# First FFN products on half tiles over four column blocks, and attention of batch 1 behind the w3@w_out blocks

## The chip, the cores and the metric

The kernel runs on one core of a Trainium2 chip. The metric is the time of one execution on the device in microseconds; the medians are over the runs given with them. A profiled execution also has a *span*, from its first to its last instruction, which is about 2 us shorter than its time. The kernel before takes 260.06 us; the execution whose profile is read here took 259.7 us (span 257.9).

Engine names in the profile: PE is TensorE (matmuls and transposes), PEld its weight loads, DVE is VectorE, ACT is ScalarE, POOL is GpSimd, SP is SyncE. L344 is line 344 of that kernel's own file, so one line of code has different numbers in different kernels.

## The reference

```python
# attention, for each of 8 batches and 8 heads; S = 576, D = 64
phi(x) = concat(relu(x) * cos(theta), relu(x) * sin(theta))     # 128 features
kv  = phi(k)^T @ v            # 128 x 64
z   = sum_s phi(k)            # 128
x   = (phi(q) @ kv) / (phi(q) @ z + 1e-6)
# FFN on 4608 tokens: model width 512, inner width 1024
out = ((x @ w1) * (x @ w2) @ w3) @ w_out
```

Inputs and outputs are float32; the kernel computes in bf16 and folds `w3 @ w_out` into one 1024 x 512 matrix, w34, while it runs. The FFN works on tiles of 512 tokens, nine in all: tile 0 needs four of the five chunks of queries of batch 0, and tile 1 needs the fifth and chunks of batch 1.

## The kernel before

Each chunk of 128 queries goes through a chain of three engines: q transpose (PE), copy, numerator (PE), normalisation (DVE), x transpose (PE), copy to xT (ACT). Ahead of it, DVE makes the cosine half and ACT the sine half of phi (`qp` in the profile). The sums `kv` and `z` of a batch are copied out of PSUM into `kvs`, half by ACT and half by DVE, before its first numerator.

```python
def num(b, c):                       # numerator and normalisation of one chunk
    ...
    for h in range(H):
        nc.tensor.matmul(nt[:, h // 4, ds((h % 4) * 65, 65)], lhsT=qpT[:, h, ds(at, 128)],
                         rhs=kvs[:, h, :], start=True, stop=True)
    nc.vector.tensor_scalar_add(out=den[rows], in0=n4[:, :, :, 64], scalar1=1e-6)
    nc.vector.reciprocal(out=den[rows], in_=den[rows])
    nc.vector.tensor_tensor(out=xblk[rows], in0=n4[:, :, :, 0:D], in1=den..., op=ALU.mult)

def x_tr(b, c):                      # for batches 0 and 1
    for kc in range(4):
        nc.tensor.transpose(pst[:, kc, 0:R], xf[:, ts(kc, 128)], identb[rows, rows])
    nc.scalar.copy(out=xT[t][:, :, ds(o, R)], in_=pst[:, 0:4, 0:R])
```

The FFN is a generator that stops after each group of four 512-column matmuls (0.865 us of PE). Whatever lies in the slot of that number is emitted there, so a slot number is a place in PE's instruction order. Tile 0 has 24 slots; the eight w3@w_out blocks, two halves each, lie in slot 15 and have places 0 to 15 of their own, after which places 16 to 23 are the output groups of tile 0. The parts that the change touches:

```python
if t == 0:                           # first products: two column blocks, token quarters
    for group in (((0, 0),), ((0, 1), (1, 0)), ((1, 1), (0, 2), (1, 2)), ((0, 3), (1, 3))):
        ...
for jp in range(4): load_w3(jp)      # loads: batch 1 lies between the blocks of w3
load(1, "k"); load_w3(4); load(1, "v"); load_w3(5); load(1, "q"); load_w3(6); load_w3(7)
...
attention_at(1, between, kv=(7, 8, 8, 9, 9), tr=(10, 11, 13, 15, 17),
             nu=(12, 14, 16, 18, 20), xt=(14, 16, 18, 20, 22))
```

In the last line, `nu` are the places of the five numerators and `xt` those of the five x transposes: each transpose is two places behind its numerator.

## Time and profile before

| stage of the kernel before | from | to | what happens in it |
|---|---|---|---|
| start | 0 | 9.78 us | loads, idle matmuls (the first 7 start 0.43 us apart, the later ones 0.216) |
| opening | 9.78 | 21.15 us | attention of batch 0; PE waits for other engines |
| rest of tile 0 | 21.15 | 65.62 us | FFN, w3@w_out, attention of batch 1; PE without gaps |
| tile 1 | 65.62 | 84.05 us (products) | FFN, attention of batch 2; PE without gaps |
| tiles 1 to 8 | 84.05 | 257.9 us | the same, in steady state |

PE sets the time: 96% busy, and 91% of the chain that ended last. The prediction below shows these lines and the chain of the opening. Two more lines of the timeline of the kernel before are needed as marks. Columns are start, length, engine, line, operation, output and inputs, shapes, and a bracket with idle time and its releaser if PE was idle before it.

```profile
35.77 0.61 PE L199 MATMUL pst<-identb,w3b 128*128 128x128 bf16 x8
...
65.62 1.03 PE L391 MATMUL ffnps<-xT,w1b 128*128 128x512 bf16 x4
```

The first is the transpose of the second w3 block (call it the **w3 mark**: all first FFN products lie ahead of it), the second the first product of tile 1 (the **tile 1 mark**). Comparing these two marks between kernels tells in which stage time was won or lost. One caution: a kernel that leaves some of this work for behind a mark reaches the mark earlier by as much. The changed kernel leaves the numerator and the x transpose of chunk 3 of batch 1 (0.26 + 0.22 us of PE) to tile 1.

### The profile page before, as it was taken

The numbers are of one execution on the slowest core, as the hardware profiler recorded it, in microseconds if no ns is written. First come the engines' busy times: TensorE is split into PE (matmuls) and PEld (weight loads), VectorE is DVE, ScalarE is ACT, GpSimd is POOL, SyncE is SP. The second block draws the span as 40 slices with busy tenths as digits, with TensorE's granted clock in tenths as the row PEclk, the third lists the DMA queues.
The fourth block names the chain that finished last, engine by engine and source line by source line (L and its number), as shares of the span: only waits on it lengthen the run. The fifth ranks groups of instructions, "written<-read, shape, count | busy, mean of one in ns | idle before, by whom it ended". The sixth has DMA issues, their size and how long they took to land.

```text
span 257.9 us, 5056 instructions
## 1 busy us (share of the span) xinstructions
PE 248.3 (96%) x1954; PEld 134.0 (52%) x1954; DVE 147.0 (57%) x344; ACT 128.3 (50%) x219; POOL 84.3 (33%) x144
## 2 busy tenths in 40 slices
PE   8778999999999999999999999999999999999992
PEld 3467455665555455546554654555455544444442
DVE  6785557569699538834972687178516613313320
ACT  2765327639955546545655465646533233323322
POOL 7752244440690374048205900610140031022000
PEclk9999999999999999999999999999999999999999
DMA  7999999999599999988998999826490252014015
GB/s 194 184 196 206 210 201 203 201 198 199 165 153 178 152 170 190 165 164 147 195 160 173 173 198 124 185 62 122 93 205 11 46 123 78 0 37 128 0 43 122
DMA packets 66968, 37.10 MB, mean 144 GB/s; under 512 B 35584, under 2 KB 63488, under 8 KB 66944
## 3 DMA queue, kind: packets, MB, share of 16 engines
q0 software_dynamic: 34432, 27.20, 64.5%
q1 hardware_dynamic: 32352, 9.44, 20.7%
q8 instruction: 15, 0.25, 0.4%
q10 hardware_dynamic: 160, 0.13, 0.2%
q14 instruction: 9, 0.07, 0.1%
HBM read 38.80 MB, written 9.44 MB: 187 GB/s over the span
## 4 chain that ended last, share of the span: by engine, by line
PE 91%; DMA 3%; DVE 2%; ACT 1%; issue 1%; ACTq 0%; POOLq 0%
PE ffnps L391 47%; PE ffnps L421 23%; PE ffnps L211 5%; PE pst L297 4%; PE pnum L315 4%; PE pnum L268 3%; DMA vs<-in_v_dram 3%; PE pst L199 1%; DVE xblk L322 1%; PE pst L344 1%; DVE qpT L299 1%; PE ffnps L438 0%; PE kva L285 0%; ACT osb L440 0%; DVE den L320 0%
## 5 line engine op out<-in xcount | busy, mean ns | idle before, releaser
L416 DVE TENSOR_TENSOR abT<-asb,ffnps 128x512 bf16<-128x512 bf16 x70 | 47.8, 683 | 69.7 <-PE ffnps L391 66.4
L391 PE MATMUL ffnps<-xT,w1b 128*128 128x512 bf16 (+1 forms) x312 | 74.9, 362 | 0.7 <-DVE xblk L322 0.6
L391 PE MATMUL ffnps<-xT,w2b 128*128 128x512 bf16 (+1 forms) x312 | 74.9, 362 | 0.0
L412 ACT CAST asb<-ffnps 128x512 bf16<-128x512 f32 x70 | 41.0, 586 | 64.8 <-PE ffnps L391 57.9
L421 PE MATMUL ffnps<-w34b,abT 128*128 128x512 bf16 x280 | 63.7, 379 | 0.0
L383 POOL DMA_DIRECT2D out_dram<-osb x42 | 22.3, 536 | 122.5 <-ACT osb L427 122.5
L391 PEld LDWEIGHTS <-w1b 128*128 128x128 bf16 x312 | 28.0, 98 | 28.4 <-issue 1.0
L421 PEld LDWEIGHTS <-abT 128*128 128x128 bf16 x280 | 26.7, 98 | 30.2
L391 PEld LDWEIGHTS <-w2b 128*128 128x128 bf16 x312 | 26.9, 97 | 23.9
L427 ACT COPY osb<-ffnps 128x512 f32<-128x512 f32 x35 | 20.5, 585 | 36.6 <-PE ffnps L421 36.6
L244 ACT ACTIVATE qp<-qs,sinv 128x512 bf16<-128x512 bf16 (+1 forms) x40 | 28.4, 721 | 0.8 <-DMA qs<-in_q_dram 0.8
L322 DVE TENSOR_TENSOR xblk<-pnum,den 128x512 bf16<-128x512 f32 (+1 forms) x38 | 26.2, 691 | 1.3
L244 ACT ACTIVATE kp<-ks,sinv 128x512 bf16<-128x512 bf16 (+1 forms) x35 | 24.7, 721 | 0.0
L315 PEld LDWEIGHTS <-qpT 128*128 128x128 bf16 x320 | 15.1, 98 | 8.0 <-DVE qpT L299 0.3
L242 DVE TENSOR_SCALAR qp<-qs,cosv 128x512 bf16<-128x512 bf16 (+1 forms) x40 | 18.5, 474 | 0.3 <-DMA qs<-in_q_dram 0.3
L260 POOL COPY va<-vs 128x512 bf16<-128x512 bf16 (+1 forms) x30 | 18.6, 645 | 0.0
L299 DVE COPY qpT<-pst 128x1024 bf16<-128x1024 bf16 (+1 forms) x22 | 13.7, 626 | 5.0 <-PE pst L297 4.7
L315 PE MATMUL pnum<-kvs,qpT 128*128 128x65 bf16 x304 | 16.0, 194 | 0.0
L297 PEld LDWEIGHTS <-qp 128*128 128x128 bf16 x192 | 12.5, 98 | 6.6 <-ACT qp L244 1.8
L211 PE MATMUL ffnps<-woutb,w3T 128*128 128x512 bf16 x64 | 15.8, 379 | 0.0
L268 PEld LDWEIGHTS <-kp 128*128 128x128 bf16 x280 | 12.9, 98 | 5.4
L297 PE MATMUL pst<-identb,qp 128*128 128x128 bf16 x192 | 14.6, 219 | 1.1 <-ACT qp L244 0.5
(73 smaller groups left out, 174.0 us busy)
## 6 DMA issues: line engine op xcount, KB each, us to landing
out_dram<-osb POOLq DMA_DIRECT2D x16, 256.0 KB, 3.4
out_dram<-osb POOLq DMA_DIRECT2D x24, 128.0 KB, 3.1
qs<-in_q_dram POOLq DMA_DIRECT2D x9, 256.0 KB, 7.7
ks<-in_k_dram POOLq DMA_DIRECT2D x7, 320.0 KB, 6.3
vs<-in_v_dram POOLq DMA_DIRECT2D x7, 320.0 KB, 8.3
qs<-in_q_dram POOLq DMA_DIRECT2D x7, 320.0 KB, 6.8
w3b<-in_moe_w_dram POOLq DMA_DIRECT2D x8, 256.0 KB, 15.3
ks<-in_k_dram POOLq DMA_DIRECT2D x7, 256.0 KB, 7.0
```

What stands on the lines that cost most here:

```text
L211: nc.tensor.matmul(acc[:, :], lhsT=w3T[:, lc, :], rhs=woutb[:, lc, :], start=(lc == 0), stop=(lc == 7))
L244: nc.scalar.activation(out=dst[:R, c, :, D:F], in_=src[:R, :, c, :], func=ACTF.Relu, scale=sinv[:R, at:at + 1], bias=0.0)
L268: nc.tensor.matmul(kvt[:, h // 4, ds((h % 4) * 65, 65)], lhsT=kp[:, c, h, :], rhs=va[:, c, h, 0:D + 1], start=(i == 0 and h % 4 == 0), sto ...
L297: nc.tensor.transpose(pst[:, h, :], qp[:, c, h, :], identb[:])
L315: nc.tensor.matmul(nt[:, h // 4, ds((h % 4) * 65, 65)], lhsT=qpT[:, h, ds(at, 128)], rhs=kvs[:, h, :], start=True, stop=True)
L322: nc.vector.tensor_tensor(out=xblk[rows], in0=n4[:, :, :, 0:D], in1=den[rows].unsqueeze(3).to_broadcast([R, 2, 4, D]), op=ALU.mult)
L383: on.dma_start(out=rows[:, :, cols], in_=osb[64 * i:64 * i + rows.shape[0], :, cols])
L391: nc.tensor.matmul(out_ps[:, tok], lhsT=w[:, kc, ts(jc, 128)], rhs=x[:, kc, tok], start=(kc == 0), stop=(kc == 3))
L412: nc.scalar.copy(out=asb[:], in_=aT[:, :])
L416: nc.vector.tensor_mul(out=abT[:, jc, :], in0=asb[:], in1=bT[:, :])
L421: nc.tensor.matmul(ops[:, :], lhsT=abT[:, jc, ts(ms, 128)], rhs=w34b[:, jc, :], start=(jc == 0), stop=(jc == 7))
L427: nc.scalar.copy(out=osb[:, ms % 2, :], in_=ops[:, :])
```

## The change

The intent: let the first FFN product start as soon as one chunk of tokens is normalised, cover the waits for later chunks with more products (four column blocks instead of two, on half tiles of 256 tokens), and get attention of batch 1 out of the way of the w3@w_out blocks, so that those need only w3 itself. Its core, with cuts (the comments are the document's):

```diff
-    idle_mms(28)
+    idle_mms(31)
 ...
-    for jp in range(4):
+    for jp in range(8):
         load_w3(jp)
-    load(1, "k")
-    load_w3(4)
-    load(1, "v")
-    load_w3(5)
-    load(1, "q")
-    load_w3(6)
-    load_w3(7)
+        if jp == 4:
+            load(1, "k")
+    load(1, "qv")
 ...
         if t == 0:
-            acc = [ps_ffn.tile([P, 512], FP32, name="ffnps") for _ in range(4)]
-            for group in (((0, 0),), ((0, 1), (1, 0)), ((1, 1), (0, 2), (1, 2)), ((0, 3), (1, 3))):
-                ...
-        for jc in range(2 if t == 0 else 0, 8):
+            yield from on_half(0)       # per half: column blocks 0, 1 in quarters of 128 tokens,
+            yield from on_half(1)       # then blocks 2, 3 on 256 tokens
+        for jc in range(4 if t == 0 else 0, 8):
 ...
-            spread(prep_units(1, (prep_k,)), 2, 4, between)
-            spread(prep_units(1, (prep_v,)), 5, 7, between)
-            spread(prep_units(1, (prep_q,)), 8, 11, between)
-            attention_at(1, between, kv=(7, 8, 8, 9, 9), tr=(10, 11, 13, 15, 17),
-                         nu=(12, 14, 16, 18, 20), xt=(14, 16, 18, 20, 22))
+            spread(prep_units(1, (prep_k,)), 8, 10, between)
+            spread(prep_units(1, (prep_q,)), 13, 15, between)
+            spread(prep_units(1, (prep_v,)), 15, 16, between)
+            attention_at(1, between, kv=(16, 16, 17, 17, 18), tr=(14, 15, 15, 16, 17),
+                         nu=(19, 20, 21, 22, 24), xt=(20, 21, 22, 23, 25))
 ...
-            spread(prep_units(2), 17, 23, slots)
+            spread(prep_units(2, (prep_k,)), 20, 23, slots)
+        elif t == 1:
+            # the rest of batch 1's attention, batch 2's q and v preparation in slots 0 to 4,
+            # batch 2's attention and batch 3's preparation a little later than before
```

Not shown: the order of the chunks' instructions ahead of the FFN (the sine half of chunk 0 goes before the kvs copy, idle matmuls stand elsewhere, the numerators use other PSUM pools), and the products' output banks.

More of the change, by code (lines that the diff above doesn't have):

```diff
@@ L96 @@
     ps_tr = ctx.enter_context(tc.tile_pool(name="ps_tr", bufs=2, space=bass.MemoryType.PSUM))
-    first = ctx.enter_context(ExitStack())
-    ps_first = first.enter_context(tc.tile_pool(name="ps_first", bufs=1, space=bass.MemoryType.PSUM))
+    first = [ctx.enter_context(ExitStack()) for _ in range(2)]
+    ps_idle = first[1].enter_context(tc.tile_pool(name="ps_idle", bufs=1, space=bass.MemoryType.PSUM))
+    ps_first = first[0].enter_context(tc.tile_pool(name="ps_first", bufs=1, space=bass.MemoryType.PSUM))
     ctx.enter_context(tc.manual_schedule())
@@ L159 @@
     nc.scalar.activation(out=tiny[:], in_=zeros[:, 0:1], func=ACTF.Relu, scale=1.0, bias=0.0)
-    unread = ps_first.tile([P, 512], FP32, name="unread")
-    kva = ps_first.tile([P, 512], FP32, name="kva")
+    unread = ps_idle.tile([P, 512], FP32, name="unread")
+    kva = ps_idle.tile([P, 512], FP32, name="kva")
     def idle_mms(n):
@@ L175 @@
     load_first(nc.gpsimd, q0, q, 2, 2)
-    for c0, n in ((0, 256), (256, 256), (512, 512)):
+    for c0, n in ((0, 256), (256, 256), (512, 256), (768, 256)):
         nc.gpsimd.dma_start(out=w1b[:, :, ds(c0, n)], in_=w1v[:, :, ds(c0, n)])
         nc.gpsimd.dma_start(out=w2b[:, :, ds(c0, n)], in_=w2v[:, :, ds(c0, n)])
-        if c0 == 0:
+        if c0 == 256:
             load_first4(nc.gpsimd, q0, q)
     nc.gpsimd.dma_start(out=woutb[:], in_=moe_w_out.rearrange("(c p) m -> p c m", p=P))
-    for jp in range(4):
+    for jp in range(8):
         load_w3(jp)
-    load(1, "k")
-    load_w3(4)
-    load(1, "v")
-    load_w3(5)
-    load(1, "q")
-    load_w3(6)
-    load_w3(7)
+        if jp == 4:
+            load(1, "k")
+    load(1, "qv")
     load(2, "kqv")
@@ L207, in w34_mm @@
         if part == 0:
-            w34_acc[jp] = ps_ffn.tile([P, 512], FP32, name="ffnps")
+            w34_acc[jp] = ffn_tile()
         acc, w3T = w34_acc[jp], w3Ts[jp]
@@ L237, in att_of, with features @@
         return att[b]
-    def features(b, dst, src, c):
+    def features(b, dst, src, c, cos=True, sin=True):
         R = ROWS[c]
         at = c if b == 0 else NCH + c
-        nc.vector.tensor_scalar(out=dst[:R, c, :, 0:D], in0=src[:R, :, c, :], scalar1=0.0,
-                                scalar2=cosv[:R, at:at + 1], op0=ALU.max, op1=ALU.mult)
-        nc.scalar.activation(out=dst[:R, c, :, D:F], in_=src[:R, :, c, :], func=ACTF.Relu,
-                             scale=sinv[:R, at:at + 1], bias=0.0)
+        if cos:
+            nc.vector.tensor_scalar(out=dst[:R, c, :, 0:D], in0=src[:R, :, c, :], scalar1=0.0,
+                                    scalar2=cosv[:R, at:at + 1], op0=ALU.max, op1=ALU.mult)
+        if sin:
+            nc.scalar.activation(out=dst[:R, c, :, D:F], in_=src[:R, :, c, :], func=ACTF.Relu,
+                                 scale=sinv[:R, at:at + 1], bias=0.0)
     def prep_k(b, c):
@@ L287, in kv_first @@
                                  stop=(c == NCH - 1 and h % 4 == 3))
+        att_of(0)["kvs"] = kvs
+        yield
         nc.scalar.copy(out=kvs[:, 0:4, :], in_=halves[0][:, 0:260])
         nc.vector.tensor_copy(out=kvs[:, 4:8, :], in_=halves[1][:, 0:260])
-        att_of(0)["kvs"] = kvs
+        yield
     def q_tr(b, c, evac=True):
@@ L309, in num @@
         qpT, kvs = att[b]["qpT"], att[b]["kvs"]
-        if b == 0 and c in (0, 2):
+        if b == 0 and c == 0:
             nt = ps_first.tile([P, 2, 512], FP32, name="pfirst")
@@ L383, in store, with ffn_tile @@
             on.dma_start(out=rows[:, :, cols], in_=osb[64 * i:64 * i + rows.shape[0], :, cols])
+    ffn_tiles = [0]
+    def ffn_tile():
+        pool = ps_ffn[ffn_tiles[0] // 2 % 2]
+        ffn_tiles[0] += 1
+        return pool.tile([P, 512], FP32, name="ffnps")
     def ffn_groups(t):
@@ L387, in ffn_groups, with products @@
         abT = fsb.tile([P, 8, 512], BF16, name="abT", bufs=2)
-        def products(out_ps, w, jc, tok):
+        def products(out, w, jc, tok):
             for kc in range(4):
-                nc.tensor.matmul(out_ps[:, tok], lhsT=w[:, kc, ts(jc, 128)], rhs=x[:, kc, tok],
+                nc.tensor.matmul(out, lhsT=w[:, kc, ts(jc, 128)], rhs=x[:, kc, tok],
                                  start=(kc == 0), stop=(kc == 3))
-        def to_abT(jc, aT, bT):
-            asb = fsb.tile([P, 512], BF16, name="asb")
-            nc.scalar.copy(out=asb[:], in_=aT[:, :])
-            nc.vector.tensor_mul(out=abT[:, jc, :], in0=asb[:], in1=bT[:, :])
@@ L399, in ffn_groups @@
-        if t == 0:
-            acc = [ps_ffn.tile([P, 512], FP32, name="ffnps") for _ in range(4)]
-            for group in (((0, 0),), ((0, 1), (1, 0)), ((1, 1), (0, 2), (1, 2)), ((0, 3), (1, 3))):
-                for jc, quarter in group:
-                    products(acc[2 * jc], w1b, jc, ts(quarter, 128))
-                    products(acc[2 * jc + 1], w2b, jc, ts(quarter, 128))
-                    if quarter == 3:
-                        to_abT(jc, acc[2 * jc], acc[2 * jc + 1])
-                yield
@@ L408, in ffn_groups, with on_half @@
-        for jc in range(2 if t == 0 else 0, 8):
-            aT = ps_ffn.tile([P, 512], FP32, name="ffnps")
-            products(aT, w1b, jc, slice(0, 512))
+        def on_half(half):
+            for pair in range(2):
+                a, b = ffn_tile(), ffn_tile()
+                if pair == 0:
+                    for quarter in range(2):
+                        for i in range(2):
+                            for ps, w in ((a, w1b), (b, w2b)):
+                                products(ps[:, ds(256 * i + 128 * quarter, 128)], w, i,
+                                         ds(256 * half + 128 * quarter, 128))
+                            if half == 0 and quarter == 0 and i == 0:
+                                yield
+                        if quarter == 0:
+                            yield
+                else:
+                    for ps, w in ((a, w1b), (b, w2b)):
+                        for i in range(2):
+                            products(ps[:, ts(i, 256)], w, 2 + i, ts(half, 256))
+                asb = fsb.tile([P, 512], BF16, name="asb")
+                nc.scalar.copy(out=asb[:], in_=a[:, :])
+                nc.vector.tensor_mul(out=abT[:, ts(pair, 2), ts(half, 256)],
+                                     in0=asb[:].rearrange("p (i n) -> p i n", i=2),
+                                     in1=b[:, :].rearrange("p (i n) -> p i n", i=2))
+                yield
@@ L411, in ffn_groups @@
+        if t == 0:
+            yield from on_half(0)
+            yield from on_half(1)
+        for jc in range(4 if t == 0 else 0, 8):
+            aT = ffn_tile()
+            products(aT[:, :], w1b, jc, slice(0, 512))
             asb = fsb.tile([P, 512], BF16, name="asb")
@@ L413, in ffn_groups @@
             yield
-            bT = ps_ffn.tile([P, 512], FP32, name="ffnps")
-            products(bT, w2b, jc, slice(0, 512))
+            bT = ffn_tile()
+            products(bT[:, :], w2b, jc, slice(0, 512))
             nc.vector.tensor_mul(out=abT[:, jc, :], in0=asb[:], in1=bT[:, :])
             yield
+        if t == 0:
+            yield
         for ms in range(3 if t == NT - 1 else 4):
-            ops = ps_ffn.tile([P, 512], FP32, name="ffnps")
+            ops = ffn_tile()
             for jc in range(8):
@@ L435, in ffn_groups @@
                 cols = ts(half, 256)
-                ops = ps_ffn.tile([P, 512], FP32, name="ffnps")
+                ops = ffn_tile()
                 for jc in range(8):
@@ L456 @@
         prep_v(0, c)
-    kv_first()
-    for c in range(2):
-        prep_q(0, c)
+    kv_steps = kv_first()
+    next(kv_steps)
+    prep_q(0, 0)
+    next(kv_steps)
+    prep_q(0, 1)
     idle_mms(2)
     q_tr(0, 0)
-    q_tr(0, 1)
-    for c in range(2, 4):
-        prep_q(0, c)
-    idle_mms(1)
+    prep_q(0, 2)
+    q_tr(0, 1, evac=False)[1]()
     num(0, 0)
-    q_tr(0, 2, evac=False)[1]()
-    idle_mms(1)
-    q_tr3 = q_tr(0, 3, evac=False)[1]
+    features(0, feat[0][1], raw[0, "q"], 3, sin=False)
+    idle_mms(3)
+    x_tr(0, 0)
     num(0, 1)
-    idle_mms(2)
-    x_tr(0, 0)
-    q_tr3()
-    num(0, 2)
-    x_tr(0, 1)
-    feature_buffers(1)
-    first.close()
-    ps_ffn = ctx.enter_context(tc.tile_pool(name="ps_ffn", bufs=4, space=bass.MemoryType.PSUM))
+    features(0, feat[0][1], raw[0, "q"], 3, cos=False)
+    q_tr(0, 2)
+    ps_ffn = []
+    for stack in first:
+        stack.close()
+    for i in range(2):
+        ps_ffn.append(ctx.enter_context(tc.tile_pool(name=f"ps_ffn{len(ps_ffn)}", bufs=2,
+                                                     space=bass.MemoryType.PSUM)))
     for t in range(NT):
@@ L482 @@
         if t == 0:
-            slots[0].append(lambda: num(0, 3))
-            slots[0].append(lambda: x_tr(0, 2))
-            slots[1].append(lambda: x_tr(0, 3))
-            slots[1].append(lambda: prep_q(0, 4))
-            slots[4].append(lambda: q_tr(0, 4))
-            slots[7].append(lambda: num(0, 4))
-            slots[9].append(lambda: x_tr(0, 4))
-            slots[14].append(lambda: w3_tr(0))
-            between = [[] for _ in range(32)]
-            spread(prep_units(1, (prep_k,)), 2, 4, between)
-            spread(prep_units(1, (prep_v,)), 5, 7, between)
-            spread(prep_units(1, (prep_q,)), 8, 11, between)
-            attention_at(1, between, kv=(7, 8, 8, 9, 9), tr=(10, 11, 13, 15, 17),
-                         nu=(12, 14, 16, 18, 20), xt=(14, 16, 18, 20, 22))
+            slots[0].append(lambda: x_tr(0, 1))
+            slots[1].append(lambda: num(0, 2))
+            slots[1].append(lambda: q_tr(0, 3, evac=False)[1]())
+            slots[2].append(lambda: x_tr(0, 2))
+            slots[2].append(lambda: num(0, 3))
+            slots[3].append(lambda: x_tr(0, 3))
+            slots[4].append(lambda: feature_buffers(1))
+            slots[5].append(lambda: prep_q(0, 4))
+            slots[7].append(lambda: q_tr(0, 4))
+            slots[9].append(lambda: num(0, 4))
+            slots[11].append(lambda: x_tr(0, 4))
+            slots[13].append(lambda: w3_tr(0))
+            between = [[] for _ in range(32)]
+            later = [[] for _ in range(24)]
+            spread(prep_units(1, (prep_k,)), 8, 10, between)
[3 more added lines that the diff above has]
+                         nu=(19, 20, 21, 22, 24), xt=(20, 21, 22, 23, 25))
+            later[:8] = between[24:32]
             for jp in range(8):
@@ L505 @@
             slots[16].append(lambda: load(3, "kqv"))
-            spread(prep_units(2), 17, 23, slots)
+            spread(prep_units(2, (prep_k,)), 20, 23, slots)
+        elif t == 1:
+            for g in range(24):
+                slots[g] += later[g]
+            spread(prep_units(2, (prep_q,)), 0, 4, slots)
+            spread(prep_units(2, (prep_v,)), 0, 4, slots)
+            attention_at(2, slots, kv=(2, 3, 4, 5, 6), tr=(3, 5, 7, 9, 11),
+                         nu=(8, 10, 12, 14, 17), xt=(8, 10, 12, 14, 17))
+            for g, name in ((1, "k"), (8, "q"), (15, "v")):
+                slots[g].append(lambda name=name: load(4, name))
+            each = [u for c in zip(*(prep_units(3)[i:i + NCH] for i in (0, 5, 10))) for u in c]
+            spread(each, 6, 23, slots)
         else:
```

## The prediction

> **What bounds the kernel now.** I read the page first (engine shares, the slices, the chain that ended last), then busy time in stretches I chose, then the timeline of the first 28 us and of the passage from token tile 0 to token tile 1. The two ends of the page say that TensorE (PE) is the bound:
>
> ```profile
> span 257.9 us, 5056 instructions
> PE 248.3 (96%) x1954; PEld 134.0 (52%) x1954; DVE 147.0 (57%) x344; ACT 128.3 (50%) x219; POOL 84.3 (33%) x144
> ...
> PE 91%; DMA 3%; DVE 2%; ACT 1%; issue 1%; ACTq 0%; POOLq 0%
> ```
>
> Busy PE is not yet full PE, so I cut the span at the last visible gap of the opening (21.15 us) and at the starts of tiles 1 and 2. Columns: stretch, its length, then busy time of PE, weight loads, DVE, ACT, POOL, clock, DMA.
>
> ```profile
> 9.78:21.15 11.37, 8.54 (x147) 6.80 (x146) 9.32 (x28) 6.70 (x11) 5.85 (x9) 1.00 1.51 195
> 21.15:65.62 44.47, 44.38 (x412) 26.73 (x413) 28.43 (x67) 24.85 (x44) 15.62 (x24) 1.00 1.31 204
> 65.62:84.05 18.43, 18.43 (x178) 10.77 (x177) 15.51 (x33) 12.49 (x23) 8.92 (x15) 1.00 1.02 158
> ```
>
> After 21.15 PE has almost no gap, and the work there is issued at full rate: eight 512-column matmuls of w3@w_out start at 36.21 and the next group at 37.94, so 1.73/8 = 216 ns each. In 9.78 to 21.15 PE idles 2.8 us and another 2 us of its busy time is idle matmuls on zeros or overlap of modelled ends. So this change has two questions: how many of these early microseconds it recovers, and whether it opens gaps in a stretch that has none. The waits of the opening are a latency chain per chunk of queries, seen in the timeline (start, length, engine, line, instruction):
>
> ```profile
> 15.68 0.42 PE L315 MATMUL pnum<-kvs,qpT 128*128 128x65 bf16 x8
> ...
> 16.13 0.17 DVE L319 TENSOR_SCALAR den<-pnum 128x8 f32<-128x8 f32 x1 [0.41 <-PE pnum L315]
> ...
> 16.34 0.20 DVE L320 RECIPROCAL den<-den 128x8 f32<-128x8 f32 x1
> ...
> 16.57 0.69 DVE L322 TENSOR_TENSOR xblk<-pnum,den 128x512 bf16<-128x512 f32 x1
> ...
> 18.45 0.38 PE L391 MATMUL ffnps<-xT,w1b 128*128 128x128 bf16 x4 [0.64 <-DVE xblk L322]
> ...
> 21.15 0.40 PE L344 MATMUL pst<-identb,xblk 128*128 128x128 bf16 x4 [0.72 <-DVE xblk L322]
> ```
>
> The reader should see that the numerator (L315) starts at 15.68 and its normalised block is complete at 16.57+0.69 = 17.26: 1.58 us, of which PE needs 0.26 us. A transpose of that block (L344) can start some 0.05 us later. Call this 1.64 us the **normalisation latency**. In tile 0's later half the kernel before hides it by putting two groups of other matmuls between numerator and transpose:
>
> ```profile
> 57.69 0.42 PE L315 MATMUL pnum<-kvs,qpT 128*128 128x65 bf16 x8
> ...
> 58.59 0.69 DVE L322 TENSOR_TENSOR xblk<-pnum,den 128x512 bf16<-128x512 f32 x1
> ...
> 58.81 0.61 PE L297 MATMUL pst<-identb,qp 128*128 128x128 bf16 x8
> ...
> 59.26 1.03 PE L421 MATMUL ffnps<-w34b,abT 128*128 128x512 bf16 x4
> ```
>
> There the next transpose comes at 60.12, 2.43 us after the numerator.
>
> **What the Trainium skill says.** "TensorE: Matmul & The Clock Gate", section "Back-to-back issue gap", gives N/2.4 + 2.5 ns per warm matmul. The trace agrees: 216 ns at 512 columns, and 128-column groups of four follow each other by 0.225 us, 56 ns each. For 256 columns, an estimate from this page is 109 ns. (The page's other figure, 131 ns at 512 columns in a sustained stream, isn't what this trace shows.) So half tiles cost PE nothing: two of 109 for one of 216. The same page, "What's actually happening", says that the clock falls back only after an idle window of about 3.4 us; gaps of up to 1 us before left the granted clock at 1.00, and I expect no new gap over 1.5 us, so no slow clock. "Perfetto Trace Analysis", "Optimization Strategy", says that an equal gap repeating on the engine that should be saturated can mean too few buffers. I expect repeating gaps here, but from latency, not only from the single pnum buffer.
>
> **The opening.** I walked the changed order with durations of the timeline before. Landing of the first two q chunks stays 11.26 (issued 3.56, 7.7 to landing), so little moves before that. The sine half of chunk 0 now precedes the kvs copy on ACT: 11.31 to 12.02, first q transpose at 12.08 (before 12.21). Its copy is done 13.42, numerator 0 at 13.45 (13.61). DVE no longer has a second qpT copy and two cosine halves ahead of it (the den began only at 14.60): den 13.98, block 0 complete 15.11 (before 15.73). Transpose 15.16 (16.36), ACT copy 15.59 to 16.18. Numerator 1 at 15.39 and q transpose 2 fill PE to 16.10. The first FFN product now needs only chunk 0 and a PSUM bank of the idle pool, not the bank that waited for xblk: it starts at 16.22 instead of 18.45.
>
> From there gaps return: 0.35 us for transpose 1 (block 1 complete 16.97), about 0.1 for numerator 3, 0.37 for transpose 3. Issue time: six groups of 128-column products for two blocks x two halves, two pairs of 256-column groups of 1.73 us. I get column blocks 0 to 3 ended at 25.77. Before, blocks 0 to 3 ended at 27.72 but with q transpose 4 (0.45 us) in it. Gain: 27.72 - 0.45 - 25.77 = **1.5 us**. The small weight blocks (512 KB of fp32 source each, about 1.3 us apart by the landings before) arrive in time: blocks 0 by 15.4, 1 by 18.0, 2 by 21, 3 by 24. Three more idle matmuls before 9.78 end before the v data lands and cost nothing. The 0.21 us gap before transpose 4 (29.91 before) may go too: 0.1 to 0.2.
>
> **Attention of batch 1.** w3 and the products before it no longer depend on k, q, v of batch 1. Loads: w3 complete near 43, q near 46, v near 48.8 us, against needs of 47, 48 and 52; no wait on DMA. PE issues the same matmuls, so nothing is saved, but order creates waits:
> - q transpose of its chunk 4 comes one half block (0.865 us) after w3@w_out group 6. ACT first copies that group, then makes the sine half: 0.2 + 0.48 + 0.73 = 1.41 us. Gap 0.55.
> - the kvs copy: DVE's half waits for ACT's (49.10 after 48.70+0.37 in the trace), so about 1.35 us from the last kv group to the numerator, with 0.26+0.865 of PE work in it. Gap 0.23.
> - numerators in output groups 19, 20, 21, 22 and each transpose one group later. PE has 0.26+0.865 = 1.125 us between, the latency is 1.64. Gap 0.52 each, for chunks 4, 0, 1, 2 and, one slot into tile 1, chunk 3: 5 x 0.52 = 2.6.
> - the transpose of chunk 2 is now the last thing before tile 1's first product, which reads it. From transpose start to ACT copy complete 0.43+0.60 = 1.03, minus 0.22 of issue: gap 0.8. Before, this copy was two groups earlier.
>
> Sum 4.2 us. Batch 2's preparation in tile 1 (ACT 3.6 us of sine halves in five slots) I expect to fit in the four-deep PSUM rotation. Tiles 2 to 8 are the same program and merely shift.
>
> **Total.** 260.08 - 1.5 - 0.1 + 4.2 = 262.7. I shade it to **262.2**, as a gap can be shorter where weight loads and queues let PE run ahead, and the opening's gain could be nearer 2.
>
> **Rivals.** (a) The opening dominates: gain 2 to 2.5 us because DVE or ACT run less queued than in my walk, and new gaps total under 1.5 us. For it: the program before has a 46.62 wait on the q load in its w3 stretch, so an earlier FFN without the move would have hit a DMA wait, and the move looks designed for this. Against it: the one-group distance is plain in the instruction order. It would give 258.5 to 259.5. (b) Attention is worse than computed: DVE's key features (about 0.3 each) or ACT's in between delay den or the xT copy by another 0.3 to 0.5 per chunk, and ACT's load at the start of tile 1 holds up the PSUM rotation. In the trace DVE halves its rate while POOL copies va (three cosine halves took 1.93 us at 64.06). It would give 264 to 265. (c) The DMA stream holds PE: w3 block 7 or a small weight block late by a microsecond, 263 to 264; the landings before leave 3 to 4 us of room, so unlikely.
>
> **Range and chances.** Main case 0.6, (a) 0.25, (b) and (c) 0.15. Range 258.8 to 263.9. 2% is 5.2 us, more than the whole gap of the opening (11.37 us minus 6.4 of real work, about 5), so faster by 2% needs everything: 0.01. Slower by 2% needs new gaps of 6.7 us: 0.03.
>
> **What would show it.** Right: first FFN product at 16 to 16.5, products of four blocks ended near 25.8, PE busy without gap until the w3 stretch ends near 50; then five gaps of about 0.5 us before x transposes with DVE xblk as releaser, and one of 0.8 before tile 1 with ACT xT; tile 1 starts some 2 us later than 65.62 less one chunk's 0.5. Wrong: gaps before x transposes absent or under 0.3 (the latency or its filler misjudged), FFN start at 17 or later, or waits on DMA in the w3 stretch.

## The result, and the profile after

The changed kernel takes 262.96 us (262.63 to 263.02, four runs) against 260.06 us of the kernel before. The ratio is 1.0107, with a 95% interval of 1.009 to 1.0125: 1.1% slower, well inside 2%. Every ratio here is the mean time of one kernel's runs over that of the other's of the same rounds, so it is not quite the ratio of the medians quoted.

The page after, answering to the first lines shown of before:

```profile
span 261.2 us, 5061 instructions
PE 249.4 (96%) x1939; PEld 135.2 (52%) x1972; DVE 144.6 (55%) x344; ACT 128.4 (49%) x219; POOL 85.2 (33%) x146
...
PE 91%; DVE 4%; ACT 1%; issue 1%; ACTq 0%
```

PE is still 96% busy and 91% of the chain, so the page alone hides the story. What changed in the last line is that DMA is gone from the chain and that DVE has doubled, from 2% to 4%. The stretches say where (columns as in the prediction: stretch, length, then busy time of PE, weight loads, DVE, ACT, POOL, clock, DMA):

```profile
22.31:51.12 28.81, 28.18 (x224) 16.84 (x228) 15.66 (x33) 12.61 (x23) 11.79 (x18) 1.00 1.28 204
51.12:67.51 16.39, 14.07 (x162) 8.62 (x166) 10.30 (x29) 9.96 (x19) 3.90 (x6) 1.00 1.31 205
67.51:87.03 19.52, 19.00 (x186) 11.08 (x188) 15.40 (x37) 12.66 (x22) 8.79 (x15) 1.00 0.90 134
```

Before, PE was busy 44.38 of 44.47 us from the end of the opening to tile 1. Now it loses 2.3 us (16.39 - 14.07) in 51.12 to 67.51 alone, at a granted clock of 1.00; the starts below show that this is still too little. The timeline of the opening shows the first FFN product at 16.60, where it was 18.45:

```profile
15.53 0.40 PE L345 MATMUL pst<-identb,xblk 128*128 128x128 bf16 x4 [0.58 <-DVE xblk L323]
...
16.60 0.38 PE L399 MATMUL ffnps<-xT,w1b 128*128 128x128 bf16 x4
...
17.41 0.40 PE L345 MATMUL pst<-identb,xblk 128*128 128x128 bf16 x4 [0.20 <-DVE xblk L323]
```

Column blocks 0 to 3 end at 26.07 us, and the w3 mark comes at 34.45 instead of 35.77: a lead of 1.32 us. This is the timeline of the changed kernel from the end of the w3 stretch to the start of tile 1:

```profile
51.12 0.62 PE L298 MATMUL pst<-identb,qp 128*128 128x128 bf16 x8 [0.43 <-ACT qp L243]
...
61.02 0.43 PE L316 MATMUL pnum<-kvs,qpT 128*128 128x65 bf16 x8
61.29 1.03 PE L445 MATMUL ffnps<-w34b,abT 128*128 128x512 bf16 x4
...
61.93 0.69 DVE L323 TENSOR_TENSOR xblk<-pnum,den 128x512 bf16<-128x512 f32 x1
...
62.68 0.40 PE L345 MATMUL pst<-identb,xblk 128*128 128x128 bf16 x4 [0.36 <-DVE xblk L323]
...
64.56 0.40 PE L345 MATMUL pst<-identb,xblk 128*128 128x128 bf16 x4 [0.36 <-DVE xblk L323]
...
66.43 0.40 PE L345 MATMUL pst<-identb,xblk 128*128 128x128 bf16 x4 [0.36 <-DVE xblk L323]
...
67.51 1.02 PE L399 MATMUL ffnps<-xT,w1b 128*128 128x512 bf16 x4 [0.67 <-ACT xT L346]
```

Follow one round. The numerator starts at 61.02, one output group follows at 61.29, and PE could go on at 61.29 + 0.865 = 62.155. The normalised block is complete only at 61.93 + 0.69 = 62.62, and its transpose starts at 62.68. The gap is 0.53 us. The bracket says 0.36 because the listed length of a group, 1.03 us, is 0.17 longer than the 0.865 us after which the next group starts when nothing holds it. All gaps below are worked out in this way, from starts.

The chain that ended last, in order of time, passes through DVE in every round (start, length, engine and work; "issue" is time that waited for nothing visible). Before, PE went through this stretch without DVE:

```profile
61.93 0.70 DVE xblk L323
62.63 0.05 issue
62.68 0.40 PE pst L345 x4
63.07 0.27 PE pnum L316 x8
```

The ledger from start to end:

| place | gained or lost | working |
|---|---|---|
| to the w3 mark | -1.32 | 34.45 - 35.77 |
| q transpose of chunk 4, 51.12 | +0.59 | PE free at 47.94 + 12 x 0.216 = 50.53 |
| kvs copy, numerator at 59.19 | +0.22 | PE free at 58.10 + 0.865 |
| x transposes at 60.80, 62.68, 64.56, 66.43, 70.01 | +2.58 | 0.48, 0.53, 0.53, 0.52, 0.52 |
| first product of tile 1, 67.51 | +0.85 | PE free at 66.43 + 0.23 |
| end of tile 1 | +0.26 | numerator at 85.90 late by 0.15 (it waits for DVE's xblk multiply); one abT multiply late by 0.11 |
| sum | +3.18 | |

The first long run of output matmuls in tile 1 starts at 89.29 us against 86.19, and from there every mark is late by the same 3.10 us to the last outputs (254.59 against 251.49). So the ledger is complete to 0.1 us up to there. It compares two single executions, whose spans differ by 3.3 us (261.2 - 257.9); 0.2 of this lies behind the last outputs. The medians differ by 2.90, as the profiled execution of before (259.7 us) was faster than the median it is compared with.

### The profile page after: what moved, and what is told of

It is laid out like the page before. It is cut to its first block, busy times and chain, and to the rows that moved or that the text cites. A ratio compares the mean times of both kernels' runs of the same rounds, so it can differ in the third digit from the quotient of the medians.

```text
span 261.2 us, 5061 instructions
## 1 busy us (share of the span) xinstructions
PE 249.4 (96%) x1939; PEld 135.2 (52%) x1972; DVE 144.6 (55%) x344; ACT 128.4 (49%) x219; POOL 85.2 (33%) x146
## 4 chain that ended last, share of the span: by engine, by line
PE 91%; DVE 4%; ACT 1%; issue 1%; ACTq 0%
PE ffnps L399 46%; PE ffnps L445 21%; PE ffnps L208 5%; PE pnum L316 4%; PE pst L298 4%; PE unread L168 4%; PE pnum L267 3%; DVE xblk L323 2%; PE pst L196 1%; PE pst L345 1%; DVE den L321 1%; DVE den L320 1%; PE ffnps L462 0%; ACT kvs L272 0%; ACT osb L464 0%
## 5 line engine op out<-in xcount | busy, mean ns | idle before, releaser
L438 DVE TENSOR_TENSOR abT<-asb,ffnps 128x512 bf16<-128x512 bf16 x68 | 46.4, 683 | 65.8 <-PE ffnps L399 65.2
L399 PE MATMUL ffnps<-xT,w1b 128*128 128x512 bf16 (+2 forms) x312 | 74.2, 357 | 1.2 <-ACT xT L346 0.7
L399 PE MATMUL ffnps<-xT,w2b 128*128 128x512 bf16 (+2 forms) x306 | 73.2, 357 | 0.5
L434 ACT CAST asb<-ffnps 128x512 bf16<-128x512 f32 x68 | 39.8, 585 | 64.1 <-PE ffnps L399 56.7
L399 PEld LDWEIGHTS <-w1b 128*128 128x128 bf16 x320 | 28.8, 97 | 27.6 <-issue 0.8
L323 DVE TENSOR_TENSOR xblk<-pnum,den 128x512 bf16<-128x512 f32 (+1 forms) x39 | 26.9, 691 | 1.3
L240 DVE TENSOR_SCALAR qp<-qs,cosv 128x512 bf16<-128x512 bf16 (+1 forms) x40 | 16.2, 413 | 0.6 <-DMA qs<-in_q_dram 0.6
L208 PE MATMUL ffnps<-woutb,w3T 128*128 128x512 bf16 x62 | 14.9, 379 | 0.1
```

The costliest lines, as they stand in the source:

```text
L208: nc.tensor.matmul(acc[:, :], lhsT=w3T[:, lc, :], rhs=woutb[:, lc, :], start=(lc == 0), stop=(lc == 7))
L399: nc.tensor.matmul(out, lhsT=w[:, kc, ts(jc, 128)], rhs=x[:, kc, tok], start=(kc == 0), stop=(kc == 3))
L434: nc.scalar.copy(out=asb[:], in_=aT[:, :])
L438: nc.vector.tensor_mul(out=abT[:, jc, :], in0=asb[:], in1=bT[:, :])
```

## The experiments

All kernels below gave correct results. Those with three or five rounds were timed beside the kernel before on the same chip.

### Each half of the change alone

**The opening alone.** The changed kernel with the load order, the places of batch 1's attention and the preparation of batch 2 of the kernel before:

```diff
+    for jp in range(4): load_w3(jp)
+    load(1, "k"); load_w3(4); load(1, "v"); load_w3(5); load(1, "q"); load_w3(6); load_w3(7)
-    for jp in range(8): ...
+            attention_at(1, between, kv=(7, 8, 8, 9, 9), tr=(10, 11, 13, 15, 17),
+                         nu=(12, 14, 16, 18, 20), xt=(14, 16, 18, 20, 22))
-        elif t == 1: ...
```

> The changed kernel with the load order after w_out, the attention of batch 1 and the preparation slots of the kernel before: the new opening alone. My theory (opening gains about 1.3 us, the move loses about 4.3): 258.8 us, PE lead at the second w3 transpose about 1.3 us as in the changed kernel (34.45 against 35.77), and kept to the end. Rival (the move was needed, without it the earlier PE runs into the loads of v and q of batch 1 and of w3): PE waits on DMA, or on features that wait for DMA, in 42 to 52 us, time 259.5 to 260.5.

Measured: 259.68 us (259.63 to 259.73), ratio 0.9993 (0.9978 to 1.0008), no difference that can be told from none. The theory expected about 1.3 us of gain and the rival, that later loads eat it, is what happened. The w3 mark comes at 34.37, a lead of 1.40 us, and then the timeline of this run shows

```profile
44.01 0.62 PE L200 MATMUL pst<-identb,w3b 128*128 128x128 bf16 x8 [0.52 <-DMA w3b<-in_moe_w_dram]
...
47.75 0.62 PE L200 MATMUL pst<-identb,w3b 128*128 128x128 bf16 x8 [0.39 <-DMA w3b<-in_moe_w_dram]
```

PE arrives earlier at w3 blocks that don't land earlier. From starts, 0.69 us (43.06 + 0.26 to 44.01) and 0.54 us go here, and the remaining 0.16 by the last w3 transpose. (The expectation of the reordered kernel below has the first of these as its bracket, 0.52, and so the rest as 0.3.) There the kernel is level with the kernel before (50.99 against 50.97), and so it is at the tile 1 mark (65.64 against 65.62).

**The attention alone.** The kernel before with the changed load order, places and preparation:

```diff
-    for jp in range(4): ...
+    for jp in range(8):
+        load_w3(jp)
+        if jp == 4: load(1, "k")
+    load(1, "qv")
+            attention_at(1, between, kv=(16, 16, 17, 17, 18), tr=(14, 15, 15, 16, 17),
+                         nu=(19, 20, 21, 22, 24), xt=(20, 21, 22, 23, 25))
```

> The kernel before with only the moved attention of batch 1, its load order and its preparation slots: the old opening. My theory, parts add up: 260.06 plus 4.25 of new gaps plus about 0.2 at the end of tile 1, so 264.4 us. Rival (the new gaps are partly an effect of the earlier opening, since features and loads have then less time): under 263 us.

Measured: 264.51 us (264.47 to 264.88), ratio 1.0182 (1.0167 to 1.0198). This is 4.64 us over the 259.87 us of the kernel before in that job. The same gaps stand in its trace 2 us later, with the same brackets (the one before tile 1 at 69.49, 0.67). So the move costs 4.6 us by itself. The opening takes back 1.7 of these in the whole change (4.64 - 2.90, each over the kernel before of its own job), but only 0.19 us without the move: the two halves are not additive. The two waits on w3 in the run before say why: with the old load order the blocks that PE reaches earlier have not landed.

### Are the gaps latency?

**Filler in the gaps.** Two extra 512-column matmuls (0.43 us) in four of the places between numerator and transpose, 8 x 0.216 = 1.73 us of PE work in all; each repeats the first matmul of a group, whose later start overwrites it, so the result is unchanged:

```diff
+    for _ in range(2 if t == 0 and ms >= 2 and jc == 0 else 0):      # and likewise in
+        nc.tensor.matmul(ops[:, :], lhsT=abT[...], rhs=w34b[...], start=True, stop=True)   # two more places
```

> The changed kernel with eight more full 512-column matmuls (two in front of w3@w_out group 7, two in front of each of the third and fourth output of tile 0, two in front of the first w2 product of tile 1; each repeats the group's first matmul, which starts the sum anew, so the result is the same), 8 x 0.216 = 1.73 us of TensorE work, placed in four of the gaps. My theory, TensorE waits there for ACT or VectorE and not for its own work: the gaps absorb it, time 262.9 to 263.0. Rival (these gaps are an effect of what TensorE has to do before): 264.6.

Measured: 262.88 us (262.65 to 263.08), ratio 1.0108 (1.0094 to 1.0122), the changed kernel's own time. 1.73 us of added PE work cost nothing. In its timeline the filler stands in front of the group, and the transpose follows without a bracket:

```profile
59.18 0.59 PE L452 MATMUL ffnps<-w34b,abT 128*128 128x512 bf16 x2
59.61 1.03 PE L454 MATMUL ffnps<-w34b,abT 128*128 128x512 bf16 x4
60.57 0.29 PE L348 MATMUL pst<-identb,xblk 64*128 64x64 bf16 x4
```

The numerator was at 58.92, so the distance to the transpose is 1.65 us; in the changed kernel, without filler, it was 60.80 - 59.19 = 1.61. So up to 0.43 us of work per gap is free, and PE's work there is not what sets the pace.

**A shorter chain.** Batch 1's reciprocal reads the denominator straight from PSUM, without the addition of 1e-6 (the result is within tolerance):

```diff
+        if b == 1:
+            nc.vector.reciprocal(out=den[rows], in_=n4[:, :, :, 64])
```

> The changed kernel without the addition of 1e-6 for batch 1, so that each normalisation is shorter by one VectorE instruction of about 0.2 us (result the same to rounding). My theory, latency from numerator to transpose sets five gaps: each shrinks from about 0.52 to 0.31, time lower by about 1.0 us, 261.9. Rival (the gaps come from queue or buffer and not from this latency): no change, 262.9.

Measured: 261.88 us (261.65 to 262.86), ratio 1.0075 (1.0058 to 1.0092), 2.01 us over the kernel before of its job where the changed kernel has 2.90, so about 0.9 us less. One instruction of 0.17 us and its handover is gone from each chain, and the brackets shrink from 0.36 to

```profile
63.17 0.40 PE L348 MATMUL pst<-identb,xblk 128*128 128x128 bf16 x4 [0.16 <-DVE xblk L326]
```

From starts the five gaps shrink from 2.58 to 1.61 us in sum. The profiled execution is the slowest of the four (262.86 us): it has the shorter gaps too, but started late, with its first FFN product at 17.46. Filler and shorter chain together show that the gaps before the x transposes are the latency numerator to normalised block.

**Numerators one place earlier.** kv chunks, numerators and transposes of batch 1 move up so that the transpose of chunk 2 is one group away from the start of tile 1; the distance numerator to transpose stays one group:

```diff
-            attention_at(1, between, kv=(16, 16, 17, 17, 18), ... nu=(19, 20, 21, 22, 24), xt=(20, 21, 22, 23, 25))
+            attention_at(1, between, kv=(16, 16, 16, 17, 17), ... nu=(18, 19, 20, 21, 24), xt=(19, 20, 21, 22, 25))
```

> The changed kernel with kv, numerators and transposes of chunks 4, 0, 1, 2 of batch 1 one output group earlier, so that one output group stands between the last transpose and the first product of tile 1. My theory: only the gap of 0.85 us before tile 1 closes, 262.1 us; the gaps of about 0.5 before the transposes stay. Rival (that gap is hidden or comes back as another wait): 262.7 to 263.0.

Measured: 261.91 us (261.82 to 262.08), ratio 1.008 (1.0065 to 1.0095), 2.04 us over the kernel before of its job, so about 0.9 us less than the changed kernel. Two waits are gone from its timeline:

```profile
57.99 0.42 PE L316 MATMUL pnum<-kvs,qpT 128*128 128x65 bf16 x8
...
66.34 1.03 PE L399 MATMUL ffnps<-xT,w1b 128*128 128x512 bf16 x4
```

The first is the wait of 0.22 us for the kvs copy, as a q transpose and a group now stand behind the last kv chunk; the second is the wait of 0.85 us before tile 1. The five before x transposes remain with the same 0.34 and 0.36. So the wait before tile 1 belongs to the place of the last transpose. The two come to 1.07 us; the medians show a little less.

**Fewer idle matmuls.** The changed kernel with 28 instead of 31 of them:

```diff
-    idle_mms(31)
+    idle_mms(28)
```

> The changed kernel with 28 idle matmuls at the start, as before, not 31. In the changed kernel's profile they end at 10.7 and the first kv matmul follows at 10.77, while its v block was ready near 9.85; the first q transpose came at 12.48, its features were ready at 12.1. My theory: 0.3 to 0.4 us less, 262.6. Rival (the clock's warm-up or the q landing decides, the three matmuls do nothing): 262.9.

Measured: 262.73 us (262.57 to 263.32), ratio 1.0107 (1.0093 to 1.012), the changed kernel's own ratio. No effect can be told from the runs' own spread. How long the idle matmuls take differs by run: 7 slow ones (0.43 us apart) in the trace before, 14 in the trace after. That agrees with the Trainium skill ("TensorE: Matmul & The Clock Gate", section "What's actually happening"), by which the same kernel has a different number of cold matmuls from run to run.

What moves the start of an execution more is when q lands: ACT's first sine half, released by that load, starts at 11.38 us in the trace after, at 12.00 in this run's and at 12.55 in that of the shorter chain. The last two executions (263.32 and 262.86 us) are each the slowest of their four.

### Can both halves be had without the gaps?

**Reordered.** The opening alone, with v of batch 1 loaded behind w3 block 5 and q behind all of w3, and attention two places later than before but with two groups between numerator and transpose:

```diff
+    for jp in range(8):
+        load_w3(jp)
+        if jp == 4: load(1, "k")
+        if jp == 5: load(1, "v")
+    load(1, "q")
+            attention_at(1, between, kv=(10, 10, 11, 11, 12), tr=(12, 13, 15, 17, 19),
+                         nu=(14, 16, 18, 20, 22), xt=(16, 18, 20, 22, 24))
```

> The opening-only kernel, with v of batch 1 loaded after w3 block 5 and q of batch 1 after all of w3, and kv, q transposes, numerators and x transposes of batch 1 placed some two slots later than in the kernel before but still two groups apart. The opening-only run lost its lead of 1.4 us to two waits on w3 loads and one more after it (0.52, 0.54 and about 0.3). My theory: with this order no wait on a load remains and no one-group distance arises, so the lead is kept: 258.7 us. Rival (the loads are simply too slow for any order, the lead is lost again): 259.6 to 260.

Measured: 260.21 us (259.92 to 260.34), ratio 1.0005 (0.9992 to 1.0017): the expected gain is missing. The waits on loads are gone, those before the transposes too but for 0.1 us before chunk 4's (which the kernel before has as well, at 54.81), and one new wait eats the lead: 1.68 us by its bracket, 1.84 from starts. PE, then ACT, in the timeline of this run:

```profile
65.96 1.02 PE L401 MATMUL ffnps<-xT,w1b 128*128 128x512 bf16 x4 [1.68 <-ACT xT L348]
```

```profile
62.53 0.58 ACT L348 COPY xT<-pst 128x512 bf16<-128x512 bf16 x1
63.00 1.35 ACT L245 ACTIVATE qp<-qs,sinv 128x512 bf16<-128x512 bf16 x2
64.24 0.58 ACT L453 COPY osb<-ffnps 128x512 f32<-128x512 f32 x1
64.70 0.74 ACT L245 ACTIVATE qp<-qs,sinv 64x512 bf16<-64x512 bf16 x1
65.33 0.58 ACT L348 COPY xT<-pst 128x512 bf16<-128x512 bf16 x1
```

The transpose of the last chunk that tile 1 needs starts at 62.78 and is over in half a microsecond, but its copy to xT runs only at 65.33. Three sine halves of batch 2's features, which are needed only in tile 1, and an output copy stand in front of it in ACT's order.

The same kernel with 28 idle matmuls:

> The same with 28 idle matmuls: by my theory another 0.3 to 0.4 less, 258.3; by the rival that they do nothing, as the reordered one.

Measured: 260.17 us (259.99 to 260.32), ratio 1.0003 (0.999 to 1.0017). The idle matmuls do nothing here either.

**Reordered, with ACT's queue cleared.** Batch 2's q and v features move from tile 0 into tile 1, as the change does, and batch 3's are spread over slots 5 to 22:

```diff
-            spread(prep_units(2), 17, 23, slots)
+            spread(prep_units(2, (prep_k,)), 17, 20, slots)
+        elif t == 1: ...                      # the changed kernel's branch
+            spread(each, 5, 22, slots)
```

> The reordered kernel with only the key features of batch 2 in tile 0's output part, and its query and value features, its attention and the features of batch 3 in tile 1, much as in the changed kernel. The reordered run had no wait on a load and no gap before a transpose, and lost its lead of 1.4 us in one gap of 1.68 before tile 1, where ScalarE was behind by ten sine halves of batch 2. My theory: with these moved the gap is gone, 258.7 to 259.0 us (up to 0.3 may come back at the end of tile 1, as in the changed kernel), below both kernels. Rival (the lead cannot be kept, something else takes it): 259.7 to 260.2.

Measured: 258.66 us (258.17 to 259.24), ratio 0.9955 (0.994 to 0.9969). Run again in a later job, the same kernel took 258.34 us (258.04 to 258.39), ratio 0.9939 (0.9926 to 0.9952). It beats both kernels, by less than 2%. The start of tile 1 in the first of these traces:

```profile
64.12 1.03 PE L401 MATMUL ffnps<-xT,w1b 128*128 128x512 bf16 x4
64.99 0.39 PE L347 MATMUL pst<-identb,xblk 128*128 128x128 bf16 x4
```

The tile 1 mark is 1.50 us earlier than before, and neither line has a bracket. Of the 1.50, 0.22 is the x transpose of chunk 3, which here stands behind the mark (64.99). The other 1.28 is nearly the whole lead of the opening (1.38 at this run's w3 mark, 34.39).

### What the half tiles are worth

**Without half tiles, first attempt.** The best kernel with the first products in the groups of the kernel before (two column blocks by four quarters):

```diff
-            yield from on_half(0)
-            yield from on_half(1)
+            for group in (((0, 0),), ((0, 1), (1, 0)), ((1, 1), (0, 2), (1, 2)), ((0, 3), (1, 3))): ...
```

> The version with kept lead, but with the first FFN products in the grouping of the kernel before (two column blocks over four quarters of tokens, then whole tiles), everything else of the new opening kept. It separates the half tiles over four column blocks from the rest of the opening (order of ScalarE and VectorE work, bank of the idle pool, start with one chunk). My theory: without column blocks 2 and 3 on the first half there is too little work while chunks 2 and 3 are normalised, a gap of about 0.8 us comes before the last quarter, the second w3 transpose starts near 35.3 where the version with kept lead has 34.39 and the kernel before 35.77, time 259.5 us. Rival (the early start alone makes the gain): second w3 transpose under 34.8, time under 259.0.

Measured: 261.18 us (260.99 to 261.72), ratio 1.0045 (1.0031 to 1.0059), much more than expected, and the edit was to blame. It left memsets of feature buffers and two multiplies on DVE ahead of the query features of chunk 4, and PE waited for those:

```profile
23.04 0.38 PE L401 MATMUL ffnps<-xT,w1b 128*128 128x128 bf16 x4 [0.67 <-ACT xT L348]
...
27.58 0.61 PE L300 MATMUL pst<-identb,qp 128*128 128x128 bf16 x8 [1.53 <-DVE qp L242]
```

The first wait is the expected one, the second an accident, so this run can't size the half tiles.

**Without half tiles, clean.** The features of chunk 4 made right after x transpose 3, the memsets behind the multiplies, chunk 4's PE work one slot later; beside it, in the same job, the best kernel once more:

```diff
-            slots[3].append(lambda: feature_buffers(1))
-            slots[3].append(lambda: prep_q(0, 4))
+            slots[2].append(lambda: prep_q(0, 4))
+            slots[4].append(lambda: feature_buffers(1))
```

> This is the reordered kernel that beat both, with the first FFN products grouped as before (two column blocks by four quarters, no half tiles), as in the run before it, but free of that run's accident: chunk 4's query features are made right after x transpose 3, ahead of the feature buffers' memsets and of the two multiplies, and chunk 4's transpose, numerator and x transpose come one slot later. Theory (half tiles cover the chain of the last quarter): TensorE waits about 0.85 us ahead of the first product of the last quarter instead of the 0.24 us of the half-tile kernel, and some 0.2 us before a numerator, and nowhere else before the w3@w_out stretch; so 0.6 to 0.9 us over the half-tile kernel, 259.3 to 259.6 us against 258.7. Rival (half tiles buy nothing, because the later work makes up for the gap): 258.6 to 258.8 us. Rival (four column blocks free of waits matter more than this trace says): 260 or more.

> The same kernel that beat both, once more beside the run without half tiles, so that the two are compared on the same chip in the same minutes: 258.2 to 259.0 us, ratio to the kernel before 0.994 to 0.997.

Measured: 259.59 us (259.21 to 260.3) without half tiles, ratio 0.9995 (0.9982 to 1.0009), against 258.34 us with them: half tiles over four blocks are worth 1.25 us. In the timelines the first FFN product starts alike (16.47 and 16.49), and the tile 1 mark lies at 65.36 and 64.08. Without half tiles the accident is gone and these waits stand there instead:

```profile
17.88 0.43 PE L318 MATMUL pnum<-kvs,qpT 128*128 128x65 bf16 x8 [0.20 <-DVE qpT L302]
...
22.59 0.38 PE L401 MATMUL ffnps<-xT,w1b 128*128 128x128 bf16 x4 [0.67 <-ACT xT L348]
...
23.70 1.02 PE L401 MATMUL ffnps<-xT,w1b 128*128 128x512 bf16 x3
```

From starts these are 0.37, 0.85 and 0.22 us (the last hidden by the listed length: by the code all four accumulator banks are held until ACT's first cast, 23.06 to 23.65). With half tiles the same stretch has one wait of 0.24 us before x transpose 3. The difference is 0.37 + 0.85 + 0.22 - 0.24 = 1.20 us; another 0.1 stands before x transpose 4, and the w3 marks lie 1.29 apart (35.63 and 34.34). The expectation had this at 0.6 to 0.9: it gave the numerator's wait as its bracket and did not see the bank.

## Why the prediction was right

The prediction, 262.2 us within 258.8 to 263.9, holds 262.96, and it named the mechanism that the runs confirm. The range reaches from below the kernel before to nearly 4 us above it, so that the time lies in it says little; what counts is that the waits stand where they were predicted, with the predicted sizes. Point by point:

- **The opening**: predicted gain 1.5 us by the end of column blocks 0 to 3, measured 27.72 - 0.45 - 26.07 = 1.2. The walk was right in its order and late by a constant: q transpose 0 was predicted at 12.08 and seen at 12.48, the first FFN product at 16.22 and 16.60. The step that failed is "three more idle matmuls ... end before the v data lands and cost nothing". In the trace after, kv matmuls start at 10.77, directly behind the idle ones, and q transpose 0 stands 0.38 us behind its sine half (11.38 + 0.72 = 12.10). It didn't matter for the time: with 28 of them neither kernel changed, and in the reordered kernel's traces q transpose 0 follows ACT at once (12.39 after 11.62 + 0.72), with the load of q as the last to come. The expected 0.1 to 0.2 more from the gap before transpose 4 is there (1.2 becomes 1.32 at the w3 mark).
- **Loads**: "no wait on DMA" is right for the changed order. The first run shows how much hangs on it: with the old order the same opening is worth 0.19 us, not to be told from nothing.
- **The gaps**: predicted 0.55, 0.23, five times 0.52, and 0.8, in sum 4.2; measured 0.59, 0.22, 2.58 and 0.85, in sum 4.24. The move alone cost 4.64, of which the gaps and the end of tile 1, as measured in the changed kernel, make 4.5. Filler, the shorter chain and the earlier places show the cause for the x transposes and for the start of tile 1. The gap of the q transpose (releaser ACT) appears as the walk has it, and filler in it was free too. The 0.22 us of the kvs copy were not tested by themselves; in the run with the places one earlier, more PE work stands in that interval and the wait is gone.
- **Tile 1**: the prediction says that batch 2's preparation fits. It nearly does: 0.26 us were lost at the end of tile 1.
- **The clock**: no slow clock, as predicted. Even the longest wait, 1.84 us in the reordered kernel, was followed by matmuls at full rate (65.96 to 66.82 for four of 512 columns).
- **The sum and the shade**: the sum was 262.7, and the shade to 262.2 went the wrong way, so that 2.1 us were forecast where 2.9 were lost. Its reason, that gaps could be shorter where queues let PE run ahead, has no example in the trace: the gaps are the computed ones to 0.05 us.
- **The rivals**: (a) a larger gain with smaller gaps did not happen; its remark that an early FFN without the move would wait on DMA is what the first run shows. (b) was wrong in tile 0, where DVE's and ACT's feature work did not lengthen the chains of the changed kernel, but the same thing cost 1.84 us in the reordered kernel. (c) did not happen.

What stays open: the whole opening with its new order of work but without half tiles was timed only in the reordered kernel, so the split of the changed kernel's own 1.3 us between half tiles (1.25 there) and the earlier start is not measured.

## What to carry to other kernels

When a dependent chain runs beside a saturated engine, its stages may stand in that engine's order only as close as the chain's latency allows: here 1.64 us between numerator and transpose, which is two groups of 0.865 us and not one. An earlier start is worth only what the next limit lets through, so after each gain look for what arrives next at that place, here a load, then a copy behind preparatory work in ACT's queue. Read such gaps from starts, as a bracket of 0.36 us stood for a gap of 0.53.

## What the Trainium skill lacked or had wrong

- "TensorE: Matmul & The Clock Gate", section "Back-to-back issue gap": it calls N/2.4 + 2.5 ns the isolated gap and gives 81 ns (128 columns) and 131 ns (512 columns) for a sustained stream. In these traces, with about one weight load per matmul, the formula is what the stream does: 56 ns (22.54 to 22.76 for four of 128 columns, after), 109 ns (16 matmuls of 256 columns from 24.33 to 26.07) and 216 ns.
- "Perfetto Trace Analysis", section "Tensor Engine Instruction (MATMUL, LD_WEIGHTS)": it says that the end of a matmul is estimated. It lacks the size of the effect: groups listed with 1.03 us are followed after 0.865, so idle time behind them is shown 0.17 us too short, and the 0.22 us bank wait of the run without half tiles isn't shown at all.
- "Perfetto Trace Analysis", section "Optimization Strategy": it says that an equal gap that repeats can mean too few buffers, and names no other cause. Here five gaps of 0.48 to 0.53 us repeat from latency and order: filler was free, a shorter chain cut each of the five by about 0.2, and one more group between left 0.1 before chunk 4 and none before the others (best kernel), all without another buffer.
- No page that I read gives the length of such a chain over engines. The chain after shows 0.02 to 0.03 us between dependent DVE instructions and 0.05 from the end of xblk to the transpose.
